# Fused attention and MoE: where in a tile's turn the scores of its last 128 keys are issued

## The chip, the cores and the metric

The kernel runs on one core of a Trainium2 chip. The metric is the device time of one execution in microseconds (us), as the median of several runs. The profile is of one execution. The engines are named as the profile names them: PE is the matrix engine, PEld its weight loads, DVE the vector engine, ACT the scalar engine, POOL the GpSimd, SP the queue that issues most transfers.

## The reference

Three layers follow one another: attention over queries that were pooled in pairs, then two MoE-like layers on its output. The change is in the attention.

```
B, H, S, D = 4, 8, 1152, 64
q_pool = q.reshape(B, H, S // 2, 2, D).mean(axis=3)          # 576 queries
scores = scale * np.matmul(q_pool, k.transpose(0, 1, 3, 2))  # 576 x 1152
scores = scores - np.max(scores, axis=-1, keepdims=True)
attn = np.exp(scores)
attn = attn / (np.sum(attn, axis=-1, keepdims=True) + 1e-09)
out = np.matmul(attn, v)
```

## The kernel before

**Tiles.** The 32 pairs of batch and head are taken two at a time: 16 steps p, each with two heads h. A step has 9 tiles t of 128 query rows. Tiles 0 to 7 are four blocks of 128 queries of each head; tile 8 holds the last 64 queries of both heads. So 144 tiles g follow each other, with p = g // 9 and t = g % 9.

**One tile.** `scores` (L74) multiplies a tile's queries with the first 1024 of its 1152 keys: two products of 512 keys, one on the upper and one on the lower 64 rows of PE, into a tile `s` of two PSUM banks, of which there are two. `scores_rest` (L88) does the last 128 keys, on the upper 64 rows, into a tile `r` of one bank, of which there is one. `maximum` (L101) has DVE take the extreme of `s` (L105) and then of `r` together with it (L112). `exps` (L115) has ACT read `r` (L123), which frees it once the row's sum has been read out, and then `s` (L125), and write the exponentials `aw_e`. `transp` (L130) turns these on PE, in 64-row halves: part 0 is 10 transposes (5 key blocks), part 1 is 8 (4 blocks). Both parts use the one tile `t` in PSUM, so part 1 can begin only when DVE has copied part 0 out (`back`, L155), and part 0 of the next tile only when ACT has copied part 1 out (L153). `push` and `av` (L194, L221) multiply the turned exponentials with the values (L203), a chunk of 8 or 12 products in each tile's turn, from a list that is filled half a step later; 8 of 9 turns of a step have such a chunk. `sums` and `sums_turn` (L159, L168) invert a half step's row sums on DVE (L164, L165) and turn them on PE (L171) into free columns of `r`. A multiplication in fp32 shows in the trace as two passes, so a score product is two rows.

**Order.** Nothing is scheduled by a tool: each piece is entered with `at(time, ...)`, where the whole part of the time is the tile's turn and the fraction the place in it, and the list is sorted and issued in that order. Each engine executes its own instructions in that order. In the turn of tile g PE has so far:

1. .0 `scores` of g
2. .15 part 1 of the transposes of g-2
3. .2 `scores_rest` of g
4. .25 the turned sums, in two turns of nine
5. .5 a chunk of the values' products
6. .98 part 0 of the transposes of g-1

DVE has in the same turn the copy of part 0 of g-2 (.1, L155), finished outputs (.11, L211, L213), one step of a background job that splits MoE weights (.12), inverted sums (.13), and the extremes of g (.6). ACT has the exponentials of g-1 (.15), the copy of part 1 of g-2 (.4), and a background step (.42). POOL adds pairs of query rows for the next step (L71, L72) as soon as their transfer has landed.

Of the kernel before, what the change touches and what calls it, by code (L numbers as in the profile page):

```python
# [29 lines left out]
def attention(tc, nc, ap, cst, xT, bg, hooks):  # L30
# [5 lines left out]
    with ExitStack() as ctx:  # L36
# [197 lines left out]
        def at(time, f, *a):  # L234
            events.append((time, len(events), f, a))
# [6 lines left out]
        for g in range(NT):  # L242
            p, t = divmod(g, NTL)
            at(g, scores, g)
            at(g + .2, scores_rest, g)
            at(g + .6, maximum, g)
            at(g + 1.15, exps, g)
            at(g + 1.98, transp, g, 0)
            at(g + 2.1, back, g, 0, "v")
            at(g + 2.15, transp, g, 1)  # L250
            at(g + 2.4, back, g, 1, "a")
            if t == 3:
                at(g + 2.13, sums, p, 0)
                at(g + 2.25, sums_turn, p, 0, g + 2)
                at(g + 4.05, spread, p, 0)
                at(g + 3.45, push, p, 0)
            if t == 8:
                at(g + 2.13, sums, p, 1)
                if g + 2 < NT:
                    at(g + 2.25, sums_turn, p, 1, g + 2)  # L260
                else:
                    at(g + 2.25, sums_last, p, 1)
                at(g + 4.05, spread, p, 1)
                at(g + 3.45, push, p, 1)
            if p + 1 < NP:
                if t in (0, 1):
                    at(g + .3 if p else g + 1.3, load_qk, p + 1, t)
                if t in (3, 4):
                    at(g + .3, prep, p + 1, t - 3, nc.gpsimd)
                if t == 6:  # L270
                    at(g + .3, load_v, p + 1)
            if t % 9 not in (3, 4, 5) and g > 3:
                at(g + .12, step, "v")
                at(g + .42, step, "a")
# [922 lines left out]
def fused(tc, q, k, v, w_in, w_sp, b_sp, w_out, w_g, w1, w2, consts, out):  # L1197
# [7 lines left out]
    with ExitStack() as ctx, tc.manual_schedule():  # L1205
# [6 lines left out]
        hooks = {"raw": lambda: m1.begin_v(keep([128, 4096], F32R, "wv").rearrange("p (n k c) -> p n k c", n=2, k=4)),  # L1212
                 "S": m1.begin, "x1": m1.begin_x1, "T": lambda: m1.split_x(0, m1.x0), "end": m1.begin_u}
        attention(tc, nc, ap, cst, xT, bg, hooks)
        bgp.close()
        tab = Pool(ctx.enter_context(tc.tile_pool(name="tab", bufs=1, side="right")), "tab")
# [77 lines left out]
```

## Time and profile before

| what | value |
|---|---|
| three runs, us | 1066.67, 1064.51, 1060.57; median 1064.51 |
| the profiled execution, us | 1063.56, its span 1061.7 |
| attention, by the first and last of its products | about 6 to 510 us of the span |
| PE busy over the span | 1008.2 us, 95% |
| DVE, ACT, POOL busy | 748.7 (71%), 595.3 (56%), 225.5 us (21%) |
| L137 on PE (transposes) | x2592, PEld idle before them 193.1 us, of which 130.3 behind DVE L155 |
| L95 on PE (scores of the last 128 keys, tiles 0 to 7) | x256, 57.2 us |
| PE clock | full in 300 to 500 us, 0.98 from 100 to 300 us |

A busy share is an average over stages: from 6 to 510 us the attention runs, behind it the other layers with other limits. The profile models where a matrix product ends, so on PE the starts of neighbouring rows say more than the lengths. A row of the timeline merges instructions of one group; its start is that of the first, its length reaches to the end of the last.

### The profile page before, as it was taken

The page shows a single profiled execution, that of the slowest core. Times are in us where ns is not written, and L with a number is a line of the kernel's source. Part 1 is how long each engine was busy: PE and PEld are TensorE (multiplying, and loading weights), DVE is VectorE, ACT ScalarE, POOL GpSimd, SP SyncE. Part 2 cuts the span into 40 slices and gives each one's busy share as a digit, 9 for nine tenths or more (in the row PEclk, how much of TensorE's full clock was granted, in tenths as well). Part 3 has the DMA queues.
Part 4 walks back from the last instruction along what each step waited for, and adds up shares of the span by engine and source line. Part 5 has one row for each costly group of instructions (what it writes and reads, how often), then busy time and mean ns, then how long its engine had stood idle before and what let it go on. Part 6 is the DMA issues. An engine that isn't in the chain of part 4 may idle for free.

```text
span 1061.7 us, 19763 instructions
## 1 busy us (share of the span) xinstructions
PE 1008.2 (95%) x7532; PEld 679.5 (64%) x7532; DVE 748.7 (71%) x1361; ACT 595.3 (56%) x1172; POOL 225.5 (21%) x189
## 2 busy tenths in 40 slices
PE   6899999999999999999879999999999999999997
PEld 3444444444544444444668988998777777777775
DVE  6787787878777787776498414232688787888884
ACT  4666666666666666666323322122277777777773
POOL 1111111111101111100355312231212321213111
PEclk9999999999999999999979999999999999999999
DMA  4444223443433343331512111001745142112840
GB/s 164 139 132 134 80 86 133 135 135 131 133 87 116 95 136 125 125 120 68 204 56 80 34 65 59 1 1 39 248 181 201 37 148 92 40 41 83 312 176 28
DMA packets 50495, 116.75 MB, mean 110 GB/s; under 512 B 8986, under 2 KB 21586, under 8 KB 48856
## 3 DMA queue, kind: packets, MB, share of 16 engines
q1 hardware_dynamic: 46672, 104.37, 29.0%
q0 software_dynamic: 3680, 11.02, 3.2%
q8 instruction: 62, 1.02, 0.4%
q14 instruction: 41, 0.34, 0.1%
q10 hardware_dynamic: 40, 0.01, 0.0%
HBM read 165.61 MB, written 19.47 MB: 174 GB/s over the span
## 4 chain that ended last, share of the span: by engine, by line
PE 75%; DVE 10%; DMA 7%; issue 4%; ACT 2%; POOL 1%; SPq 0%; POOLq 0%; DVEq 0%; ACTq 0%
PE ps_av L203 15%; PE ps_t L137 11%; PE ep_yp L1074 8%; PE ps_s L82 8%; PE ep_hp L1041 6%; DMA er_x<-x,tab_gi 4%; PE m_ps_v L626 4%; PE m_ps_u L574 4%; PE m_ps_u L560 3%; PE m_ps_v L519 3%; PE ep_hp L1034 3%; PE ps_r L95 3%; DVE aw_mx L105 2%; PE ps_s L85 2%; DMA ao_qr<-in_q 1%
## 5 line engine op out<-in xcount | busy, mean ns | idle before, releaser
L137 PEld LDWEIGHTS ps_t<-keep_ident,aw_e 64*128 64x128 f32 x2592 | 104.0, 140 | 193.1 <-DVE aw_et L155 130.3
L105 DVE TENSOR_REDUCE aw_mx<-ps_s 128x1 f32<-128x1024 f32 x144 | 174.7, 1213 | 8.3 <-ACT aw_e L125 2.5
L155 DVE COPY aw_et<-ps_t 128x640 f32<-128x640 f32 x144 | 118.5, 823 | 81.8 <-PE ps_t L137 81.5
L203 PE MATMUL ps_av<-aw_et,aw_v 128*64 128x320 f32 (+1 forms) x1152 | 168.9, 420 | 0.0
L125 ACT ACTIVATE aw_e<-ps_s,aw_mx 128x1024 f32<-128x1024 f32 x144 | 159.2, 1106 | 0.0
L137 PE MATMUL ps_t<-keep_ident,aw_e 64*128 64x64 f32 x2592 | 143.5, 235 | 15.8 <-DVE aw_et L155 12.0
L82 PE MATMUL ps_s<-ao_k,ao_q 64*128 64x512 f32 x512 | 141.7, 632 | 7.2 <-DMA ao_k<-in_k 6.0
L123 ACT ACTIVATE aw_e<-ps_r,aw_mx 128x128 f32<-128x128 f32 x144 | 53.0, 368 | 130.4 <-DVE aw_junk L112 130.4
L153 ACT ACTIVATE aw_et<-ps_t 128x512 f32<-128x512 f32 x144 | 86.0, 597 | 54.7 <-PE ps_t L137 53.4
L372 DVE TENSOR_TENSOR eb_w2l<-er_r,eb_w2h 128x1024 fp32r<-128x1024 f32 x88 | 103.5, 1217 | 4.2 <-ACT eb_w2h L368 4.1
L203 PEld LDWEIGHTS ps_av<-aw_et,aw_v 128*64 128x64 f32 x1152 | 72.0, 137 | 49.0 <-issue 4.1
L372 DVE TENSOR_TENSOR eb_w1l<-er_r,eb_w1h 128x1024 fp32r<-128x1024 f32 x66 | 78.7, 1221 | 33.6 <-ACT eb_w1h L368 33.6
L368 ACT ACTIVATE eb_w2h<-er_r 128x1024 fp32r<-128x1024 f32 x88 | 88.7, 1068 | 0.6 <-PE ep_yp L1074 0.3
L368 ACT ACTIVATE eb_w1h<-er_r 128x1024 fp32r<-128x1024 f32 x66 | 67.8, 1071 | 17.4 <-DMA er_r<-in_w 13.2
L372 POOL TENSOR_TENSOR bg_l<-bg_e,bg_h 128x256 fp32r<-128x256 f32 x16 | 11.6, 728 | 296.5 <-ACT bg_h L368 296.5
L1074 PE MATMUL ep_yp<-eb_w2h,ew_hth 128*128 128x512 f32 x176 | 71.2, 404 | 0.2 <-ACT ew_hth L368 0.2
L1074 PE MATMUL ep_yp<-eb_w2h,ew_htl 128*128 128x512 f32 x176 | 70.2, 399 | 0.2 <-DVE ew_htl L372 0.2
L1074 PE MATMUL ep_yp<-eb_w2l,ew_hth 128*128 128x512 f32 x176 | 69.1, 392 | 0.0
L1080 POOL DMA_INDIRECT out<-ew_y,tab_si x22 | 22.4, 1017 | 206.8 <-DVE ew_y L1079 183.2
L112 DVE TENSOR_SCALAR_CACHE_REDUCE aw_junk<-ps_r,aw_mx 128x128 f32<-128x128 f32 x144 | 49.9, 346 | 14.4
L71 POOL TENSOR_TENSOR ao_qr<-ao_qr 128x576 f32<-128x576 f32 x30 | 43.2, 1442 | 72.6 <-DMA ao_qr<-in_q 72.1
L95 PE MATMUL ps_r<-ao_k,ao_q 64*128 64x128 f32 x256 | 57.2, 304 | 0.0
(240 smaller groups left out, 1908.5 us busy)
## 6 DMA issues: line engine op xcount, KB each, us to landing
er_r<-in_w SPq DMA_DIRECT2D x45, 2048.0 KB
ao_qr<-in_q SPq DMA_DIRECT2D x32, 576.0 KB
ao_k<-in_k SPq DMA_DIRECT2D x32, 320.0 KB
aw_v<-in_v SPq DMA_DIRECT2D x16, 576.0 KB
xT<-aw_xo SPq DMA_DIRECT2D x16, 288.0 KB
bg_raw<-in_w_in SPq DMA_DIRECT2D x16, 256.0 KB
aw_rb<-rdram SPq DMA_DIRECT2D x64, 64.0 KB
er_r<-in_w SPq DMA_DIRECT2D x16, 256.0 KB
```

The source lines that it names most:

```text
L82: nc.tensor.matmul(d["s"][:, i, :], r["q", h][rows, 128 * n:128 * n + 128], r["k", h][rows, 0:512], start=True, stop=True)
L95: nc.tensor.matmul(d["r"][:, 0:128], r["q", h][rows, 128 * n:128 * n + 128], r["k", h][rows, 512:640], start=True, stop=True)
L105: nc.vector.tensor_reduce(out=m[:, 0:1], in_=d["s"], op=ALU.min, axis=AX.XY)
L125: nc.scalar.activation(out=e[:, 0:8, :].rearrange("p k c -> p (k c)"), in_=d["s"].rearrange("p i c -> p (i c)"), func=AF.Exp, bias=d["m"][ ...
L137: nc.tensor.transpose(t[:, i, 64 * (k - k0):64 * (k - k0) + 64], E[g]["e"][o, k, :], ident[o, o])
L153: nc.scalar.activation(out=o, in_=i, func=AF.Copy)
L155: nc.vector.tensor_copy(o, i)
L203: nc.tensor.matmul(box["t"][64 * h:64 * h + 64, 0:n], v[:, h, k, :], et[:, k, h, 0:n], start=k == 0, stop=k == 8)
L368: nc.scalar.activation(out=hi, in_=src, func=AF.Copy)
L372: (nc.gpsimd if eng_lo == "p" else nc.vector).tensor_tensor(out=lo, in0=src, in1=hi.bitcast(F32), op=ALU.subtract)
L1041: nc.tensor.matmul(pt[c], xT[xi][:, 128 * k:128 * k + 128], W1[wi][:, k, 512 * c:512 * c + 512], start=False, stop=todo[c] == 0)
L1074: nc.tensor.matmul(pt, hT[hi][:, c, 128 * o:128 * o + 128], W2[wi][:, f, :], start=f == 0 and (hi, wi) == (0, 0), stop=f == 7 and (hi, wi) ...
```

## The change

One number: in the list of places, `scores_rest` of tile g moves from .2 to .14, so that it is issued before the second part of the transposes (.15) and not behind it.

```
         for g in range(NT):
             p, t = divmod(g, NTL)
             at(g, scores, g)
-            at(g + .2, scores_rest, g)
+            at(g + .14, scores_rest, g)
             at(g + .6, maximum, g)
             at(g + 1.15, exps, g)
             at(g + 1.98, transp, g, 0)
             at(g + 2.1, back, g, 0, "v")
             at(g + 2.15, transp, g, 1)
```

Only PE's order changes. On PE, two whole turns in the second step (ps_s and ps_r are `s` and `r`, ps_t the transposes' tile, ps_av the values' products; the number at a name's end only counts tiles):

```order
 L82 MATMUL ps_s_571<-ao_k_10_156,ao_q_12_229 128x512 x2
-L137 MATMUL ps_t_579<-keep_ident_65,aw_e_544 128x64 x8
-L95 MATMUL ps_r_591<-ao_k_10_156,ao_q_12_229 128x128
+L95 MATMUL ps_r_579<-ao_k_10_156,ao_q_12_229 128x128
+L137 MATMUL ps_t_581<-keep_ident_65,aw_e_546 128x64 x8
 L203 MATMUL ps_av_551<-aw_et_294,aw_v_88 64x320 x4
-L137 MATMUL ps_t_605<-keep_ident_65,aw_e_588 128x64 x10
+L137 MATMUL ps_t_605<-keep_ident_65,aw_e_590 128x64 x10
```

The scores of the last keys now stand directly behind the other scores, and the eight transposes directly ahead of the values' products; the ten transposes at the turn's end stay.

On PE, the turn of a tile 8 in the first step, whose queries come from two heads and whose products use 64 columns instead of 128:

```order
 L85 MATMUL ps_s_382<-ao_k_2_82,ao_q_5_90 64x512
 L85 MATMUL ps_s_382<-ao_k_4_86,ao_q_6_95 64x512
-L137 MATMUL ps_t_389<-keep_ident_65,aw_e_357 128x64 x8
-L98 MATMUL ps_r_401<-ao_k_2_82,ao_q_5_90 64x128
-L98 MATMUL ps_r_401<-ao_k_4_86,ao_q_6_95 64x128
+L98 MATMUL ps_r_389<-ao_k_2_82,ao_q_5_90 64x128
+L98 MATMUL ps_r_389<-ao_k_4_86,ao_q_6_95 64x128
+L137 MATMUL ps_t_392<-keep_ident_65,aw_e_359 128x64 x8
 L203 MATMUL ps_av_321<-aw_et_138,aw_v_88 64x256 x4
```

Here the products of 64 columns, which stood on both sides of the transposes, now stand together.

On PE, a turn with turned sums (L171) and without values' products, in the second step:

```order
 L82 MATMUL ps_s_469<-ao_k_10_156,ao_q_12_229 128x512 x2
-L137 MATMUL ps_t_481<-keep_ident_65,aw_e_438 128x64 x8
-L95 MATMUL ps_r_494<-ao_k_10_156,ao_q_12_229 128x128
-L171 MATMUL ps_r_494<-keep_ident_65,aw_rs_40_478 5x128
-L137 MATMUL ps_t_516<-keep_ident_65,aw_e_491 128x64 x10
+L95 MATMUL ps_r_481<-ao_k_10_156,ao_q_12_229 128x128
+L137 MATMUL ps_t_483<-keep_ident_65,aw_e_440 128x64 x8
+L171 MATMUL ps_r_481<-keep_ident_65,aw_rs_40_478 5x128
+L137 MATMUL ps_t_516<-keep_ident_65,aw_e_493 128x64 x10
```

The turned sums keep their place ahead of the ten transposes; they now follow the eight transposes directly.

## Rows read from the trace of the kernel before

**Rows 1.** Page, part 1, PE's share, and part 2, PE's granted clock in 40 slices.
```profile
PE 1008.2 (95%) x7532; PEld 679.5 (64%) x7532; DVE 748.7 (71%) x1361; ACT 595.3 (56%) x1172; POOL 225.5 (21%) x189
...
PEclk9999999999999999999979999999999999999999
```
**Rows 2.** Page, part 5: PE's transposes; weight loads and matmuls, idle time before them.
```profile
L137 PEld LDWEIGHTS ps_t<-keep_ident,aw_e 64*128 64x128 f32 x2592 | 104.0, 140 | 193.1 <-DVE aw_et L155 130.3
...
L137 PE MATMUL ps_t<-keep_ident,aw_e 64*128 64x64 f32 x2592 | 143.5, 235 | 15.8 <-DVE aw_et L155 12.0
```
**Rows 3.** Timeline of a turn, t=4: start us, length us, instruction, [idle before <-releaser].
```profile
300.74 0.37 ACT L123 ACTIVATE aw_e<-ps_r,aw_mx 128x128 f32<-128x128 f32 x1 [0.74 <-DVE aw_junk L112]
...
300.79 0.53 PE L137 MATMUL ps_t<-keep_ident,aw_e 64*128 64x64 f32 x10
...
301.15 1.08 PE L82 MATMUL ps_s<-ao_k,ao_q 64*128 64x512 f32 x4
301.36 0.82 DVE L155 COPY aw_et<-ps_t 128x640 f32<-128x640 f32 x1 [0.71 <-PE ps_t L137]
...
302.23 0.32 PEld L137 LDWEIGHTS ps_t<-keep_ident,aw_e 64*128 64x128 f32 x8 [0.83 <-DVE aw_et L155]
302.24 0.46 PE L137 MATMUL ps_t<-keep_ident,aw_e 64*128 64x64 f32 x8
...
302.53 0.44 PE L95 MATMUL ps_r<-ao_k,ao_q 64*128 64x128 f32 x2
...
302.90 1.30 PE L203 MATMUL ps_av<-aw_et,aw_v 128*64 128x320 f32 x8
```
**Rows 4.** Timeline of PE, the same turn, short windows: the second passes alone.
```profile
301.63 0.59 PE L82 MATMUL ps_s<-ao_k,ao_q 64*128 64x512 f32 x2
...
302.70 0.27 PE L95 MATMUL ps_r<-ao_k,ao_q 64*128 64x128 f32 x1
```
**Rows 5.** Timeline of PE and PEld in a later layer: products, then transposes.
```profile
860.18 0.63 PE L1041 MATMUL ep_hp<-eb_w1h,ew_xtl 128*128 128x512 f32 x2
860.65 0.62 PE L1041 MATMUL ep_hp<-eb_w1l,ew_xth 128*128 128x512 f32 x2
861.11 0.60 PE L1022 MATMUL ep_xt<-keep_ident,er_x 128*128 128x128 f32 x4
```
**Rows 6.** Timeline of PE, turn of a tile 8.
```profile
314.49 0.53 PE L137 MATMUL ps_t<-keep_ident,aw_e 64*128 64x64 f32 x10
...
314.94 1.09 PE L85 MATMUL ps_s<-ao_k,ao_q 64*64 64x512 f32 x8
...
315.96 0.46 PE L137 MATMUL ps_t<-keep_ident,aw_e 64*128 64x64 f32 x8
...
316.35 0.44 PE L98 MATMUL ps_r<-ao_k,ao_q 64*64 64x128 f32 x4
...
316.72 1.08 PE L203 MATMUL ps_av<-aw_et,aw_v 128*64 128x256 f32 x8
```
**Rows 7.** Timeline, end of t=1 and turn of t=2.
```profile
323.70 0.27 PE L171 MATMUL ps_r<-keep_ident,aw_rs 128*5 128x128 f32 x1 [0.23 <-DVE aw_rs L165]
...
325.56 0.19 ACT L123 ACTIVATION_READ_ACCUMULATOR aw_e<-ps_r,aw_mx 128x1 f32 x1
...
325.99 0.46 PE L137 MATMUL ps_t<-keep_ident,aw_e 64*128 64x64 f32 x8 [0.65 <-DVE aw_et L155]
...
326.66 0.76 PE L203 MATMUL ps_av<-aw_et,aw_v 128*64 128x320 f32 x4
```
**Rows 8.** Timeline, turn of t=7.
```profile
311.93 0.82 DVE L155 COPY aw_et<-ps_t 128x640 f32<-128x640 f32 x1
...
312.38 0.19 ACT L123 ACTIVATION_READ_ACCUMULATOR aw_e<-ps_r,aw_mx 128x1 f32 x1
...
313.47 1.08 PE L203 MATMUL ps_av<-aw_et,aw_v 128*64 128x256 f32 x8
```
**Rows 9.** Timeline, t=1 of another step; then busy times and clock of a stretch.
```profile
104.17 1.45 POOL L71 TENSOR_TENSOR ao_qr<-ao_qr 128x576 f32<-128x576 f32 x1 [4.97 <-DMA ao_qr<-in_q]
...
104.28 1.36 DVE L164 SCALAR_TENSOR_TENSOR aw_rs<-aw_sum 128x5 f32<-128x5 f32 x1
...
108.10:111.50 3.40, 3.29 (x18) 1.69 (x18) 2.15 (x5) 2.48 (x6) 0.52 (x1) 0.50 0.10 29
```
**Rows 10.** One line of the kernel, L164: duration ns min/median/max.
```profile
L164 DVE SCALAR_TENSOR_TENSOR aw_rs<-aw_sum x32: 147/153/1360, 23.3 to 504.4; 128x4 f32<-128x4 f32 x16, 128x5 f32<-128x5 f32 x16
```

More of the change, by code (lines that the diff above doesn't have):

```diff
@@ L244, in attention @@
             at(g, scores, g)
-            at(g + .2, scores_rest, g)
+            at(g + .14, scores_rest, g)
             at(g + .6, maximum, g)
```

## Prediction

> **What bounds the kernel now.** I read the page's shares first: PE is busy 95% of the span at full clock nearly throughout [rows 1], so time must come from PE's own row or from waits that the row hides. Then the costliest groups. The transposes' weight loads stood idle 193.1 us, 130.3 of them behind L155, DVE's copy of the first ten transposes; their matmuls by the profile only 15.8, 12.0 of them behind L155 [rows 2]. The two differ because the ends of PE's rows are modelled: the scores' row reaches as far as the next row. Which is right is read from starts in a plain turn [rows 3, 4]. The scores start at 301.15, their second pass at 301.63, so a pass is 0.48 us apart, and the second should be through about 302.1. The eight transposes start at 302.24. Their copy L155 ends at 301.36 + 0.82 = 302.18, and the weight load starts 0.05 behind it. So PE stands still for some 0.1 to 0.2 us ahead of the eight transposes in a turn where the page counts almost nothing. L155 cannot come earlier: it itself waited 0.71 us for the ten transposes of 300.79.
>
> In 9 turns of a step I find three sorts. Plain ones, like rows 3: t=0, 3, 4, 5 and 6, and t=8 with another shape. Late ones, where DVE had too much before L155: t=2 (its transposes waited 0.65 us [rows 7]) and t=7 (L155 starts directly behind DVE's last instruction, with no idle time [rows 8]). And t=1, which has no values' products and ends on the turned sums, for which PE waits on DVE [rows 7].
>
> **The change, part by part.** It removes and adds no instruction and no transfer; on DVE, ACT, POOL and SP the order is as before. On PE one product of two passes goes ahead of eight transposes. I compare the stretch from the scores' start to the values' products.
>
> *Plain turn, before:* 302.90 - 301.15 = 1.75 us [rows 3].
>
> *Plain turn, after:* the first pass is 0.48. The second I take from tile 8, where the copy is not what is waited for: 315.96 - 314.94 = 1.02 for both passes there, less 0.48, less the change of shape. That change costs 0.09: the scores follow the ten transposes by 0.45 in tile 8 [rows 6] and by 0.36 in rows 3. So 0.45. The rest's first pass is 302.70 - 302.53 = 0.17; its second, by columns 128 of 512, is 0.11 [rows 4]. The transposes start at 0.48 + 0.45 + 0.17 + 0.11 = 1.21, about 0.06 less if the rest's weights load under the scores' second pass, as they cannot behind short transposes, and its first pass too takes 0.11: 1.15. That is after the copy, which allows 1.09, so the copy is no longer waited for. Eight transposes last 302.53 - 302.24 = 0.30, and the change of shape ahead of the values' products, which before stood behind the rest, is 0.09; with the weights loaded ahead the first pair is some 0.02 shorter: 0.37. In all 1.52, a gain of 0.23 us. Bounds: nothing overlaps and each pass takes 0.48 and 0.17 (1.30 + 0.39 = 1.69, gain 0.06), or the transposes start at the copy's earliest and follow directly (1.09 + 0.34 = 1.43, gain 0.32). I take 0.23, near the better end, because the one place in the trace where transposes directly follow long products shows no gap: L1041's pairs start 0.47 apart and the transposes 0.46 behind the last pair [rows 5].
>
> *A wait that the change brings forward:* the rest needs `r`, which ACT frees with L123 of the tile before. In a plain turn L123 ends at 300.74 + 0.37 = 301.11, and with the sum's readout 0.2 later; the rest would be issued at about 302.1, or 0.23 earlier when turns shrink. Some 0.6 us to spare; behind it stand the eight transposes, the copy L153 and the values' products, which all would be late with it. In late turns there is nothing to spare. *t=2:* the readout of L123 ends at 325.56 + 0.19 = 325.75; the rest follows at about 325.80, the transposes 0.28 later at 326.08 (before 325.99), the values' products 0.37 later at 326.45 against 326.66: gain 0.21, less 0.03 if the rest's second pass is long. I take 0.18; bounds 0.10 and 0.30. *t=1* gains nothing of its own, as L171 waits for DVE's sums [rows 7] wherever the rest stands. *t=6 and 7 together:* t=6 gains 0.23, but DVE gets no faster, so t=7 meets DVE and ACT where they were: readout of L123 at 312.57, rest 312.62, transposes 312.90, values 313.27 against 313.47 [rows 8]. For both 0.17; bounds 0.10 and 0.30. *t=8:* before 316.72 - 314.94 = 1.78; after 0.48 + 0.45 + 0.28 + 0.09 + 0.39 = 1.69, as one change of shape goes and one stays: 0.09; bounds 0.03 and 0.15.
>
> *Sum of a step:* t=0, 3, 4, 5 give 4 x 0.23 = 0.92, t=1 and 2 0.18, t=6 and 7 0.17, t=8 0.09: 1.36 us. Fifteen steps look alike; in the first, turns have no values' products and wait on ACT, DVE and transfers, and I count nothing. 15 x 1.36 = 20.4. The layers behind attention start from its end and shift with it. From the profiled execution, 1063.56 us (0.95 below the median of the runs), that gives 1043.2.
>
> **A rule on shapes.** The rest and the transposes both stand as 64*128 [rows 3], tile 8's products as 64*64 [rows 6], and only there does the trace show the 0.09. The Trainium skill (TensorEngine Tiling, Key Properties) says that the array drains when its tiling mode changes, not when only the tile within a mode does. By that the plain turn has no drain between rest and transposes, as I count; if each such pair cost a drain all the same, 4 x 0.09 x 15 = 5.4 us of the gain would go. No run here shows a rest directly ahead of transposes.
>
> **Rivals.**
>
> *Little overlap.* The page's own PE row has only 12.0 us of idle time behind L155 [rows 2], and part of it is in late turns such as t=2. If that is the true idle time, or the passes take their full spacing, plain turns gain 0.06 to 0.15 and a step about 0.65: 15 x 0.65 = 10, so 1053.5. For it: the page; against it: rows 3 and 4, where the passes do not fill the stretch.
>
> *DVE or ACT take over.* PE arrives earlier, but meets copies and extremes that are no faster, and turns keep their length: 1062. For it: DVE sets t=1, 2 and 7 already. Against it: in the plain turn L155 had waited 0.71 us for PE [rows 3], three times what PE gains.
>
> *Slower, by POOL.* DVE's L164 usually takes 0.15 us, but 1.36 at most [rows 10]: POOL's L71 began 0.11 us ahead of it, ran to 105.62, and L164 ended at 105.64. PE had waited, and then the clock stood at 0.50, 1.2 of 2.4 GHz, for 3.40 us [rows 9]. That is 1.2 us for the wait and at most 1.7 for the clock, 2.9 a time. L71 starts when a transfer has landed; shorter turns move L164 against it. With 10 of the 32 places of L164 hit anew the time is 1043.2 + 29 = 1072.2; it is slower than before from 8 new hits on. Against it: a start 0.1 to 0.2 us earlier takes L164 out from behind L71 in the case shown. The Trainium skill (SBUF, Who interferes with whom) states a lock between DVE and GpSimd: whichever starts first holds the shared ports for its whole instruction, against a DVE instruction with two inputs. The trace agrees, by those two ends.
>
> **How the numbers follow.** The forecast 0.65 (its own range 1033 to 1049, from 4 x 0.32 + 0.30 + 0.30 + 0.15 = 2.03 us a step at best to about 1.0); little overlap 0.17; take-over 0.10; POOL 0.08. The range to hold it 8 times in 10 reaches from 1033 to 1056, which takes in the little overlap. About 0.5%, 5.3 us, is what a measurement of this kernel can tell from no change: faster 0.65 + 0.17 = 0.82, same 0.10, slower 0.08.
>
> **What would show it.** In a plain turn the eight transposes should start 1.1 to 1.2 us after the scores with PEld's wait behind L155 nearly gone, and the values' products 1.45 to 1.55 after the scores against 1.75. In t=2 the weight load of the rest, not the transposes, should wait, and for ACT's L123. t=1 and 2 together should lose 0.2 us. DVE's wait ahead of L155 should shrink by as much as a turn. I am wrong if the transposes still start behind L155, if the rest waits for ACT in plain turns, or if L164 is long in many steps.

## The result and the profile after

| | before | changed |
|---|---|---|
| median of 6 runs, us | 1065.42 (1060.57 to 1069.78) | 1039.22 (1032.73 to 1041.95) |
| profiled execution, us | 1063.56 | 1039.24 |
| first step (first scores of step 0 to those of step 1) | 32.40 | 38.60 |
| steps 1 to 15, to the end of the last values' product | 471.76 | 440.40 |
| from the first product of the next layer on | 549.6 | 550.0 |

The ratio to before is 0.9738, 95% interval 0.9709 to 0.9767. Forecast were 1043.2 us and a range of 1033 to 1056.

The page of the changed kernel, PE's share and groups of part 5, answers to [rows 1, 2]. The weight loads of the transposes stood idle 193.1 us before, 130.3 behind the copy L155. Now they stand 66.4 us, most of it behind the other copy, L153, and the rest's weight loads have a wait of their own, for L123:

```profile
PE 981.8 (95%) x7532; PEld 695.3 (67%) x7532; DVE 745.6 (72%) x1361; ACT 594.2 (57%) x1172; POOL 228.0 (22%) x189
...
L137 PEld LDWEIGHTS ps_t<-keep_ident,aw_e 64*128 64x128 f32 x2592 | 109.6, 141 | 66.4 <-ACT aw_et L153 40.2
...
L95 PEld LDWEIGHTS ps_r<-ao_k,ao_q 64*128 64x128 f32 x256 | 47.2, 194 | 83.6 <-ACT aw_e L123 52.5
```

A plain turn of the changed kernel, from its timeline, answers to [rows 3]:

```profile
287.14 0.52 PE L137 MATMUL ps_t<-keep_ident,aw_e 64*128 64x64 f32 x10
...
287.50 1.08 PE L82 MATMUL ps_s<-ao_k,ao_q 64*128 64x512 f32 x4
...
287.71 0.82 DVE L155 COPY aw_et<-ps_t 128x640 f32<-128x640 f32 x1 [0.43 <-PE ps_t L137]
...
287.99 0.19 PEld L95 LDWEIGHTS ps_r<-ao_k,ao_q 64*128 64x128 f32 x1 [0.24 <-ACT aw_e L123]
288.41 0.38 PE L95 MATMUL ps_r<-ao_k,ao_q 64*128 64x128 f32 x2
...
288.59 0.46 PE L137 MATMUL ps_t<-keep_ident,aw_e 64*128 64x64 f32 x8
...
288.98 1.30 PE L203 MATMUL ps_av<-aw_et,aw_v 128*64 128x320 f32 x8
```

The eight transposes start 1.09 us after the scores, as before, and as before that is 0.06 us behind the end of their copy (287.71 + 0.82 = 288.53): L155 still sets their first start. What has changed is that the rest (288.41) is already in front of them, in the time in which PE stood still. The rest's weight load waits 0.24 us for L123, but ends well before its products are due, so this wait holds nothing up. From scores to values it is 288.98 - 287.50 = 1.48 us against 1.75. DVE's idle time ahead of L155 fell from 0.71 to 0.43, by the turn's gain.

The late turn t=2, from a timeline of the same kernel, answers to [rows 7]. The weight load of the rest is now what waits, for ACT, and the transposes start 1.72 after the scores as they did before (325.99, behind scores at 324.27, the line of before below); but the values' products follow 0.47 behind them and not 0.67:

```profile
324.27 1.08 PE L82 MATMUL ps_s<-ao_k,ao_q 64*128 64x512 f32 x4
```
```profile
309.46 1.08 PE L82 MATMUL ps_s<-ao_k,ao_q 64*128 64x512 f32 x4
...
310.75 0.19 ACT L123 ACTIVATION_READ_ACCUMULATOR aw_e<-ps_r,aw_mx 128x1 f32 x1
310.99 0.29 PEld L95 LDWEIGHTS ps_r<-ao_k,ao_q 64*128 64x128 f32 x2 [1.28 <-ACT aw_e L123]
...
311.18 0.27 PE L137 MATMUL ps_t<-keep_ident,aw_e 64*128 64x64 f32 x1
...
311.65 0.49 PE L203 MATMUL ps_av<-aw_et,aw_v 128*64 128x320 f32 x2
```

Turn by turn, medians of steps 1 to 14, each turn from the start of its scores to that of the next (us):

| turn t | 0 | 1 | 2 | 3 | 4 | 5 | 6 | 7 | 8 | sum |
|---|---|---|---|---|---|---|---|---|---|---|
| before | 3.56 | 2.62 | 3.97 | 3.34 | 3.34 | 4.08 | 3.13 | 3.24 | 3.16 | 30.44 |
| changed | 3.29 | 2.62 | 3.78 | 3.07 | 3.07 | 3.81 | 2.93 | 3.25 | 2.99 | 28.81 |
| gain | 0.27 | 0.00 | 0.19 | 0.27 | 0.27 | 0.27 | 0.20 | -0.01 | 0.17 | 1.63 |
| forecast | 0.23 | with t=2 | 0.18 | 0.23 | 0.23 | 0.23 | with t=7 | 0.17 | 0.09 | 1.36 |

Fifteen times 1.63 is 24.5 us. The steps gained 471.76 - 440.40 = 31.4. Most of the rest is POOL's: in the profile before, three steps were 2.7, 2.0 and 1.1 us longer than a usual one, those with an L164 of 1.36 us [rows 9, 10], and behind the first two of them PE's clock fell for 3.4 us; in the profile after no L164 lasted over 0.16, and the clock did not fall in these steps. About 1 us of the 31.4 is left without a cause. The view of the line, in the changed kernel:

```profile
L164 DVE SCALAR_TENSOR_TENSOR aw_rs<-aw_sum x32: 152/153/160, 27.5 to 479.3; 128x4 f32<-128x4 f32 x16, 128x5 f32<-128x5 f32 x16
```

Against that the first step took 6.2 us more. I had counted nothing there. The timeline of its turns shows two things. Before, the scores at 13.45 lasted 2.02 us, those from 16.95 on 1.08; and the ten transposes between them waited 0.35 us for L153:

```profile
13.45 2.02 PE L82 MATMUL ps_s<-ao_k,ao_q 64*128 64x512 f32 x4
...
16.59 0.53 PE L137 MATMUL ps_t<-keep_ident,aw_e 64*128 64x64 f32 x10 [0.35 <-ACT aw_et L153]
...
16.95 1.08 PE L82 MATMUL ps_s<-ao_k,ao_q 64*128 64x512 f32 x4
```

In the changed kernel the scores from 14.07 to 26.53 lasted 2.02 us, twice as long, in four turns. So PE's clock was at the lower of its two levels, 1.2 and not 2.4 GHz. The trace's record of the clock begins only when it first rises, 15.9 us from the timeline's zero before and 29.6 us in the changed kernel; what went before is read from the scores' length. In these turns there are no values' products, and where the rest stood in front of the ten transposes PE now stands idle 0.70 us:

```profile
17.64 0.80 PE L137 MATMUL ps_t<-keep_ident,aw_e 64*128 64x64 f32 x10 [0.70 <-ACT aw_et L153]
...
26.53 2.02 PE L82 MATMUL ps_s<-ao_k,ao_q 64*128 64x512 f32 x4
...
30.46 1.08 PE L82 MATMUL ps_s<-ao_k,ao_q 64*128 64x512 f32 x4
```

The clock did not stay up. Within the first step it fell once more, for 3.4 us before and for 6.8 us in the changed kernel; in these stretches, the first of the profile before, the third figure from the end is the granted clock:

```profile
32.98:36.39 3.41, 3.41 (x26) 1.16 (x24) 1.52 (x6) 1.55 (x4) 0.00 (x0) 0.50 0.00 1
36.39:43.22 6.83, 6.73 (x48) 3.69 (x49) 3.98 (x8) 3.29 (x8) 0.00 (x0) 0.50 0.22 80
```

So the first step had PE at the lower clock for 13.4 us before and for 30.4 us after the change.

Whether the order did that, or chance, is the first question of the experiments. The others: is L164 really held by POOL's L71; what sets the plain turn now; and does the new place pay in the late turns too.

### The profile page after: what moved, and what is told of

Same layout as the page of the kernel before. It is cut to its first block, busy times and chain, and to the rows that moved or that the text cites. A ratio compares the mean times of both kernels' runs of the same rounds, so it can differ in the third digit from the quotient of the medians.

```text
span 1037.4 us, 19763 instructions
## 1 busy us (share of the span) xinstructions
PE 981.8 (95%) x7532; PEld 695.3 (67%) x7532; DVE 745.6 (72%) x1361; ACT 594.2 (57%) x1172; POOL 228.0 (22%) x189
## 4 chain that ended last, share of the span: by engine, by line
PE 74%; DVE 11%; DMA 6%; issue 5%; ACT 3%; POOL 0%; SPq 0%; ACTq 0%; DVEq 0%; POOLq 0%
PE ps_av L203 15%; PE ps_t L137 9%; PE ep_yp L1074 9%; PE ps_s L82 8%; PE ep_hp L1041 7%; PE m_ps_v L626 5%; DMA er_x<-x,tab_gi 4%; PE m_ps_u L574 4%; PE m_ps_v L519 3%; PE ep_hp L1034 3%; PE m_ps_u L560 3%; PE ps_r L95 3%; DVE aw_mx L105 2%; PE ps_s L85 2%; PE ep_ht L1059 1%
## 5 line engine op out<-in xcount | busy, mean ns | idle before, releaser
L155 DVE COPY aw_et<-ps_t 128x640 f32<-128x640 f32 x144 | 118.4, 822 | 57.7 <-PE ps_t L137 57.4
L137 PEld LDWEIGHTS ps_t<-keep_ident,aw_e 64*128 64x128 f32 x2592 | 109.6, 141 | 66.4 <-ACT aw_et L153 40.2
L137 PE MATMUL ps_t<-keep_ident,aw_e 64*128 64x64 f32 x2592 | 148.6, 235 | 5.3 <-ACT aw_et L153 3.0
L123 ACT ACTIVATE aw_e<-ps_r,aw_mx 128x128 f32<-128x128 f32 x144 | 52.9, 367 | 121.3 <-DVE aw_junk L112 121.3
L153 ACT ACTIVATE aw_et<-ps_t 128x512 f32<-128x512 f32 x144 | 85.9, 596 | 39.3 <-PE ps_t L137 35.9
L95 PEld LDWEIGHTS ps_r<-ao_k,ao_q 64*128 64x128 f32 x256 | 47.2, 194 | 83.6 <-ACT aw_e L123 52.5
L95 PE MATMUL ps_r<-ao_k,ao_q 64*128 64x128 f32 x256 | 53.8, 291 | 8.3 <-ACT aw_e L123 7.6
```

Source lines behind the costliest of these rows:

```text
L95: nc.tensor.matmul(d["r"][:, 0:128], r["q", h][rows, 128 * n:128 * n + 128], r["k", h][rows, 512:640], start=True, stop=True)
L137: nc.tensor.transpose(t[:, i, 64 * (k - k0):64 * (k - k0) + 64], E[g]["e"][o, k, :], ident[o, o])
L153: nc.scalar.activation(out=o, in_=i, func=AF.Copy)
L155: nc.vector.tensor_copy(o, i)
```

## Experiments

Eleven runs followed, two of them of the changed kernel itself, in three groups, each group on one chip and timed beside the kernel before. Ratios are to the kernel before, with 95% intervals. "Rise" is the moment at which the trace first records PE's clock at its full level, counted from the first operation; that stands 0.25 us behind the zero of the timelines, so there a rise reads 0.25 us higher.

**The old place in the first step.** The edit to the changed kernel:

```
-            at(g + .14, scores_rest, g)
+            at(g + (.2 if g < NTL else .14), scores_rest, g)
```

> The changed kernel, but the first step (tiles 0 to 8) keeps the old place of the rest's scores. In the profile of the changed kernel the first step lasted 38.6 us against 32.4 before, at the lower clock until 29 us against 16 us. Theory A (the new order itself keeps the clock down in the first step, where turns have no values' products): the first step is back near 32.4 us, the clock full by 16 to 17 us, the time about 6 us below the changed kernel's 1039.2, so 1033. Rival B (when the clock rises is chance from run to run, whatever the order): the time stays at 1039, and the first step may last anything from 32 to 39 us.

Median 1033.85 us, ratio 0.9694 (0.9657 to 0.9730); the rise came at 16.6 us, the first step took 31.4. As theory A has it, but the interval overlaps the changed kernel's, and one profile cannot tell the order from chance.

**The new place in the first step alone.** The edit to the kernel before:

```
-            at(g + .2, scores_rest, g)
+            at(g + (.14 if g < NTL else .2), scores_rest, g)
```

> The kernel before, with the new order in the first step alone (tiles 0 to 8). Theory A: the first step lasts some 38.5 us and the time is 6 us above the kernel before, 1071.5. Rival B: no difference from the kernel before, 1065.4.

Median 1068.26 us, ratio 1.0008 (0.9974 to 1.0041): the 6 us of theory A lie outside. The rise came at 16.3 us and the first step took 32.3, in spite of the new order. So A fails as I had put it: the order does not always keep the clock down.

**Products before the first scores.** The edit to the changed kernel:

```
         load_v(0)
+        warm(nc, ps([128, 2, 512], F32, "s", bufs=2), ident, 12)
```

> The changed kernel, with 24 transposes and 36 small products of the identity issued on PE ahead of the first scores, while the first queries are still being fetched (a tile of the scores' buffer takes them and is overwritten). If the first step is long only because PE is at the lower clock there, the clock rises earlier, the first step falls below 34 us and the time to 1033 or lower. If the new order makes the first step longer at full clock too, the first step stays above 36 us and the time at 1039. If the clock falls again before the scores run, also 1039.

Median 1043.08 us, ratio 0.9772 (0.9736 to 0.9808): a miss of my own making. At the lower clock the 60 products took from 2.71 to 14.6 us, and the first scores came 8.6 us later:

```profile
2.71 1.54 PE L1190 MATMUL ps_s<-keep_ident 64*128 64x64 f32 x24 [2.71 <-DMA keep_ident<-in_consts]
4.05 5.32 PE L1193 MATMUL ps_s<-keep_ident 64*128 64x64 f32 x48
9.31 5.38 PE L1195 MATMUL ps_s<-keep_ident 128*128 128x64 f32 x24
14.62 2.08 PE L82 MATMUL ps_s<-ao_k,ao_q 64*128 64x512 f32 x4
```

Its one use: though PE issued without a gap from 2.7 us on, the rise came no earlier than 16.9. The first step, from these later first scores, lasted 31.9 us.

**One operand for the sums.** The edit to the kernel before:

```
-            nc.vector.scalar_tensor_tensor(out=rs[:, 0:n], in0=s[:, 0:n, 0], scalar=1e-9, in1=s[:, 0:n, 1], op0=ALU.add, op1=ALU.add)
+            nc.vector.tensor_reduce(out=rs[:, 0:n], in_=s[:, 0:n, :], op=ALU.add, axis=AX.X)
```

> The kernel before (old order), with the sums' first instruction L164 made from one operand: a sum over the last axis of the 2 partial sums in place of an addition of two tensors; the added 1e-9 is left out. Theory C (the 1.36 us of L164 are a wait for POOL's L71, which holds what a DVE instruction with two SBUF operands needs): no row of it lasts over 0.3 us, even where L71 runs beside it; three long turns go, and the time falls by up to 5.8 us to about 1060. Rival D (L164 waits for its operands, ACT's sums, or for the transfer that L71 also waited for): long rows stay, and the time stays at 1065.

Median 1059.45 us against 1068.01 on that chip, ratio 0.9928 (0.9899 to 0.9957). In this timeline L71 again began just before L164, as in [rows 9], by 0.07 us against 0.11 there; the view of the line has all 32:

```profile
103.10 1.42 POOL L71 TENSOR_TENSOR ao_qr<-ao_qr 128x576 f32<-128x576 f32 x1 [5.01 <-DMA ao_qr<-in_q]
103.17 0.16 DVE L164 TENSOR_REDUCE aw_rs<-aw_sum 128x5 f32<-128x10 f32 x1
```
```profile
L164 DVE TENSOR_REDUCE aw_rs<-aw_sum x32: 146/151/156, 23.9 to 499.4; 128x4 f32<-128x8 f32 x16, 128x5 f32<-128x10 f32 x16
```

With one operand L164 runs beside L71, as theory C has it. But not all of the lost time came back: steps 1 to 15 took 467.85 us against 471.76 in the profile before, 3.9 less and not 5.8. In two steps t=1 was still 1.15 and 1.01 us too long, for L71 now met L336, a background instruction of two operands just ahead of L164, which lasted 1.57 and 1.42 us instead of 0.41:

```profile
254.69 1.40 POOL L71 TENSOR_TENSOR ao_qr<-ao_qr 128x576 f32<-128x576 f32 x1 [4.65 <-PE ps_s L82]
254.80 1.57 DVE L336 SCALAR_TENSOR_TENSOR bg_e<-bg_raw,bg_e 128x256 int32<-128x256 int32 x1
```

The 8.6 us between the medians are more than that; no trace shows where the other executions gained them.

**The changed kernel again**, unchanged, beside the next three.

> The changed kernel itself, once more, beside the other three on one chip, for a second look at its first step. So far the clock rose to full at 16 to 17 us in five profiles, with the old and with the new order in the first step, and at 29 us in one, that of the changed kernel. Theory B (chance): it rises at about 16 us this time, the first step lasts near 32 us, and the profiled execution takes about 1033; over its runs the times lie in two groups some 6 us apart. Theory A (the new order): 29 us again, a first step of 38 us.

Median 1036.80 us, ratio 0.9724 (0.9677 to 0.9772). The rise came at 20.0 us and the first step took 33.6: neither theory's figure. The times, 1031 to 1046, do not fall into two groups.

**The old place in late turns.** The edit to the changed kernel:

```
-            at(g + .14, scores_rest, g)
+            at(g + (.2 if t in (2, 7) else .14), scores_rest, g)
```

> The changed kernel with the old place of the rest's scores in the two turns where DVE is late, t=2 and t=7, of every step. Theory (the new place pays there too, by taking the rest from behind the transposes, although the rest now waits for ACT): t=2 goes from 3.78 back to 3.98 us, t=7 becomes 0.2 longer, so 0.4 us a step, 15 steps, 6 us: 1045. Rival (in late turns the gain is nothing, since the rest waits for ACT about as long as the transposes waited for DVE): 1039, turns as in the changed kernel.

Median 1041.26 us, ratio 0.9754 (0.9718 to 0.9790). The difference to the changed kernel beside it, 4.5 us, is within the intervals; the turns decide. t=2 took 3.97 us against 3.78, t=7 3.45 against 3.25, so a step is 0.39 us longer, as the theory has it. In its timeline of t=2 the transposes wait for L155 and the rest stands behind them again:

```profile
75.87 1.08 PE L82 MATMUL ps_s<-ao_k,ao_q 64*128 64x512 f32 x4
...
77.47 0.46 PE L137 MATMUL ps_t<-keep_ident,aw_e 64*128 64x64 f32 x8 [0.52 <-DVE aw_et L155]
77.77 0.44 PE L95 MATMUL ps_r<-ao_k,ao_q 64*128 64x128 f32 x2
78.14 1.29 PE L203 MATMUL ps_av<-aw_et,aw_v 128*64 128x320 f32 x7
```

**Half of the values' products ahead of the rest in t=2.** The edit to the changed kernel:

```
-            for k0, k1 in ((0, 2), (2, 4), (4, 6), (6, 9)):
+            for k0, k1 in ((0, 1), (1, 2), (2, 4), (4, 6), (6, 9)) if c else ((0, 2), (2, 4), (4, 6), (6, 9)):
...
-                at(g + 3.45, push, p, 1)
+                at(g + 3.12, push, p, 1)
+                at(g + 3.135, av)
```

> The changed kernel, with half of the values' products of the turn t=2 put ahead of the rest's scores there, where PE now waits some 0.6 us for ACT to free r (to have them, the list is filled some tenths of a turn earlier). If that wait is what sets the turn, t=2 falls from 3.78 to about 3.5 us, where the copy L153, held up on ACT, becomes what the next transposes wait for: 0.3 us a step, 4.5 us in all, 1034.5. If DVE's lateness sets t=2 and 3 together whatever PE does, t=3 grows by what t=2 gains, and the time stays at 1039. It is slower if the two further changes of shape, 0.18 us, are not hidden: up to 1042.

Median 1033.76 us, ratio 0.9678 (0.9638 to 0.9718), 3 us below the changed kernel beside it, within the intervals. The turn went where expected, from 3.78 to 3.49, and what its end waits for is now L153:

```profile
77.23 1.08 PE L82 MATMUL ps_s<-ao_k,ao_q 64*128 64x512 f32 x4
...
78.24 0.76 PE L203 MATMUL ps_av<-aw_et,aw_v 128*64 128x320 f32 x4
...
79.59 0.76 PE L203 MATMUL ps_av<-aw_et,aw_v 128*64 128x320 f32 x4
79.70 0.60 ACT L153 ACTIVATE aw_et<-ps_t 128x512 f32<-128x512 f32 x1
80.35 0.39 PEld L137 LDWEIGHTS ps_t<-keep_ident,aw_e 64*128 64x128 f32 x10 [0.57 <-ACT aw_et L153]
```

In five of the steps 1 to 14 t=3 gave 0.12 to 0.25 us of it back; its median stayed at 3.07.

**Three edits together:** the first, the one of the sums and the one of the values' products.

> The changed kernel with three further edits: the old place of the rest's scores in the first step, the inverted sums made by a sum over one operand (the added 1e-9, which a float32 sum of at least 1 cannot hold, is left out), and half of the values' products of t=2 ahead of the rest. If the three add up: the first step near 32 us (about 4 us below the changed kernel on average), no long L164 (about 1 us, as the changed kernel has few), 4.5 us from t=2: 1030. If the split does nothing: 1034.

Median 1032.61 us, ratio 0.9696 (0.9657 to 0.9736), where 1030 was expected: the lowest median, but by no interval better than the changed kernel. Its profiled execution took 1029.29, with the rise at 16.7 us, a first step of 31.0 and t=2 at 3.48.

**The waits of the first step filled.** The edit to the changed kernel:

```
+        def cover():
+            t = ps([128, 512], F32, "av")
+            for i in range(6):
+                nc.tensor.transpose(t[:, 64 * i:64 * i + 64], ident[0:64, :], ident[0:64, 0:64])
...
             at(g + 2.15, transp, g, 1)
+            if g < 4:
+                at(g + 2.155, cover)
```

> The changed kernel, with six transposes of the identity, into the values' bank that is unused then, behind the second transposes of the first four tiles. In these turns of the first step there are no values' products, and since the change PE stands idle there for 0.70 us until ACT's copy L153 is through, where the rest's scores stood before. So far the clock rose at 15.7, 16.6, 16.7 and 17.1 us with the old order in the first step, and at 16.3, 18.7, 20.0, 23.9 and 29.3 us with the new. Theory (the uncovered wait for L153 keeps PE's clock down longer): filled, the clock rises by 17 us, the first step lasts 31 to 33 us, the time is some 3 us below the changed kernel's. Rival (the moment is chance): anything from 16 to 29 us, the time as the changed kernel's, 1037 to 1039.

The rise came at 15.6 us, the first step took 31.8. Median 1034.82, ratio 0.9688 (0.9661 to 0.9716). In its timeline the ten transposes wait 0.32 us for L153, where they waited 0.70. But the clock had already risen, at 15.8 us of this timeline, when the first filling transpose ran at 16.10, so the filling did not bring the rise:

```profile
16.10 0.53 PE L222 MATMUL ps_av<-keep_ident 64*128 64x64 f32 x6
16.31 0.60 ACT L153 ACTIVATE aw_et<-ps_t 128x512 f32<-128x512 f32 x1 [1.02 <-PE ps_t L137]
...
16.96 0.53 PE L137 MATMUL ps_t<-keep_ident,aw_e 64*128 64x64 f32 x10 [0.32 <-ACT aw_et L153]
17.32 1.08 PE L82 MATMUL ps_s<-ao_k,ao_q 64*128 64x512 f32 x4
```

**The changed kernel a third time**, on that chip.

> The changed kernel a third time, beside the one with filled waits and on the same chip, for one more moment of the clock's rise. Theory: later than 17 us, a first step of 33 to 39 us. Rival (chance): anything.

The rise came at 20.1 us, the first step took 33.9; two runs, 1034.31 and 1034.60, ratio 0.9689 (0.9649 to 0.9730). The filled kernel is not faster than this one.

All profiles by the order in the first step; the third column is the time from the first scores to those of step 1 that PE spent at the lower clock, before the rise and in later falls:

| order in the first step | rise, us | at the lower clock, us | first step, us |
|---|---|---|---|
| old (before; first edit; one operand; three edits) | 15.7, 16.6, 17.1, 16.7 | 13.4, 11.0, 11.5, 11.1 | 32.4, 31.4, 31.4, 31.0 |
| new (changed, three times; first step alone; halves) | 29.3, 20.0, 20.1, 16.3, 23.9 | 30.4, 17.7, 17.9, 13.6, 24.9 | 38.6, 33.6, 33.9, 32.3, 36.6 |
| new but for t=2 and 7 (old place in late turns) | 18.7 | 19.8 | 34.8 |
| new, waits filled | 15.6 | 12.7 | 31.8 |
| new, the rest doubled (below) | 17.2 | 14.8 | 33.6 |
| new, products before the first scores | 16.9 | 12.8 | 31.9 |

But for the doubled rest, every first step is 27.0 us and 0.38 us for each us at the lower clock, to within 0.4, with either order (an estimate from this table). So the new order made the first step longer only where PE was longer at the lower clock: with 13.6 us at the lower clock it took 32.3, the old one with 13.4 us 32.4.

**The rest twice.** The edit to the changed kernel, tiles 0 to 7:

```
-                nc.tensor.matmul(d["r"][:, 0:128], r["q", h][rows, 128 * n:128 * n + 128], r["k", h][rows, 512:640], start=True, stop=True)
+                for _ in range(2):
+                    nc.tensor.matmul(d["r"][:, 0:128], r["q", h][rows, 128 * n:128 * n + 128], r["k", h][rows, 512:640], start=True, stop=True)
```

> The changed kernel, with the rest's scores of tiles 0 to 7 computed twice in a row (the same products into the same place). In plain turns of the changed kernel the rest starts 0.91 us after the scores, takes 0.17, and the transposes start at 1.09, where the copy L155 also allows them. If the copy sets them and PE had time left, the transposes move by less than the 0.22 us that the second rest adds; by the 0.06 us that the weight load could have started earlier, to 1.25. If PE alone sets them, they move by the full 0.22, to 1.31. A step becomes 1.0 to 1.4 us longer, the time 15 to 20 us.

Median 1061.74 us, ratio 0.9931 (0.9903 to 0.9959): 27.3 us above the changed kernel beside it, where 15 to 20 were expected. A step was 1.3 us longer by medians, as expected, which is 19.5 us in fifteen; in the profile 5.3 us more came from the layers behind, where PE was at the lower clock for 40.7 us against 27.7. Its timeline of a plain turn (line numbers from L96 on are higher by one):

```profile
295.13 1.07 PE L82 MATMUL ps_s<-ao_k,ao_q 64*128 64x512 f32 x4
...
295.34 0.82 DVE L156 COPY aw_et<-ps_t 128x640 f32<-128x640 f32 x1 [0.65 <-PE ps_t L138]
...
296.05 0.38 PE L96 MATMUL ps_r<-ao_k,ao_q 64*128 64x128 f32 x2
...
296.22 0.27 PE L138 MATMUL ps_t<-keep_ident,aw_e 64*128 64x64 f32 x1
296.27 0.27 PE L96 MATMUL ps_r<-ao_k,ao_q 64*128 64x128 f32 x1
...
296.33 0.22 PE L138 MATMUL ps_t<-keep_ident,aw_e 64*128 64x64 f32 x1
296.38 0.27 PE L96 MATMUL ps_r<-ao_k,ao_q 64*128 64x128 f32 x1
296.39 0.50 PE L138 MATMUL ps_t<-keep_ident,aw_e 64*128 64x64 f32 x6
...
296.82 0.76 PE L204 MATMUL ps_av<-aw_et,aw_v 128*64 128x320 f32 x4
```

From scores to values it is 296.82 - 295.13 = 1.69 us, 0.21 more than in the changed kernel: the full price of the second rest. So PE has no time left over in the plain turn, and the copy no longer holds up the values' products. Yet the first transpose still starts at 1.09, neither at 1.25 nor at 1.31 as the expectation had it: again 0.06 us behind the end of the copy (295.34 + 0.82 = 296.16). Both can be true, because half of the transposes use the lower 64 rows and can start, when the copy lets them, between the passes of the rest, which uses the upper 64; the others follow the rest. That the rows at 296.22 and 296.33 are of the lower half is argued from the kernel, since the view does not name the half.

## Why the prediction was right, point by point

**What bounded the kernel** was read rightly: PE stood still ahead of the eight transposes, in turns where the page's PE row counted next to nothing. The weight loads' 130.3 us behind L155 were nearer the truth than the matmuls' 12.0 [rows 2]; a gain of 1.63 us a step could not have come out of 12.0.

**The plain turn** was mis-sized a little: 0.23 us forecast, 0.27 measured, within the bounds of 0.06 and 0.32. I let the transposes start at 1.15, behind both passes of the rest and with the copy no longer waited for. They start at 1.09, beside its second pass and 0.06 us behind the end of L155. So to the letter a sign of being wrong that I had named, transposes that still start behind L155, is there; what the copy has lost is its hold on the values' products, which the doubled rest moved by its full price. There is no sign of a drain between rest and transposes: 0.18 us lie between their starts, less than the two passes of 0.11 that stand there. The same rows refute the 0.09 us a turn that the sentence on shapes put against the forecast, and the rival of little overlap, 1053.5.

**t=1** (nothing) came as worked out, and so did the sum of **t=2** (0.18, measured 0.19), with the wait for L123 where it was put. Inside t=2 two errors cancel: the transposes start 1.72 us after the scores, where the sum had 326.08 - 324.27 = 1.81, and the values' products 0.47 behind them and not 0.37. **t=6 and 7**: 0.17 forecast, 0.19 by medians. t=6 gained 0.20 and not 0.27 for a reason I did not name: the values' products of 295.93 start 0.46 us behind the transposes and not 0.39, and 0.06 behind the end of L213, the last reader of the bank they write. The timeline of the changed kernel:

```profile
295.47 0.46 PE L137 MATMUL ps_t<-keep_ident,aw_e 64*128 64x64 f32 x8
295.66 0.21 DVE L213 TENSOR_TENSOR aw_xo<-ps_av,aw_rb 128x64 f32<-128x64 f32 x1
295.93 1.08 PE L203 MATMUL ps_av<-aw_et,aw_v 128*64 128x256 f32 x8
```

t=7 gained nothing, as DVE's lateness allows. Both late turns need the new place all the same: with the old one a step is 0.39 us longer. **t=8**: 0.09 forecast, 0.17 measured, outside its bounds of 0.03 and 0.15; by medians the rest and its change of shape took 0.32 us there where the sum had 0.37, and the scores' passes 0.91 for 0.93.

**The first step** is the term that failed: counted at nothing, it cost 6.2 us in the profiled execution. My list of what stands behind the rest named the values' products, but not the turns without any, where the rest itself had covered PE's wait for L153. The wait grew from 0.35 to 0.70 us, but it is the clock that the 6.2 us follow: 17.0 us more at the lower clock, at 0.38 each, make 6.5. Whether the order keeps the clock down is not settled. Four profiles with the old order rose at 15.7 to 17.1 us, six with the new at 16.3 to 29.3; by first steps that is some 3 us on average. Against it stands that the clock rose in two profiles, with the new order in the first step alone and with the waits filled, before the first lengthened wait or the first filling transpose. Up to there PE had the same instructions in the same order as in the three profiles of the changed kernel, which rose at 20.0 us and later, so chance has a part at least. And the new order in the first step alone showed no loss in time, filling the waits no gain.

**POOL** was the rival on the slower side, and it went the other way: the three meetings of the profile before were gone, 5.8 us that I had not put into the sum. The sentence against the rival had said why, that an earlier start takes L164 out from behind L71, but put no gain to it. For L164 the mechanism, two operands on DVE against an L71 that started first, is borne out by the kernel with one operand. The price of 2.9 us a meeting was too high on the whole: 2.7, 2.0 and 1.1 in the profile before, and 1.2 for each of two long L164 in the kernel with the new order in the first step alone, where the clock did not fall behind them. So the forecast, 1043.2 against 1039.2, holds three misses of which two nearly cancel: steps 4.1 us too small (15 x 0.27), POOL 5.8 not counted, the first step 6.2 not counted. That the total came within 4.0 us is in part luck.

**DVE or ACT take over**: not in the plain turn (the doubled rest moved it by its full price), but in t=1 and t=7, which gained nothing, as the prediction allowed.

## What to carry to other kernels

Where an instruction waits for a copy, look for independent work that stands behind it on the same engine and can go in front; size it by the starts of neighbouring rows and by the weight loads' idle time, since the matmul row hides the wait. Then go through the turns in which the moved piece had itself covered another wait, above all the first turns of a loop, where the usual work is missing. And a single long row of a short instruction is worth tracing to what ran beside it: giving L164 one operand instead of two took it out of POOL's way. Then look at its neighbours as well: in that kernel L336 was twice the long one instead, with L71 beside it, and cost 1.2 and 1.0 us.

## What the runs showed of the hardware that I had not expected

Products on the upper 64 rows of PE and transposes, by the kernel's order those of the lower 64, run beside each other in fine grain: rest passes at 296.27 and 296.38, transposes at 296.22 and 296.33. A DVE addition of two operands took 1.36 us instead of 0.15 when POOL's L71 had begun 0.11 us earlier, a sum over one operand 0.16 when it had begun 0.07 earlier. And PE's clock was first full at 16.9 us even when PE had issued products without a gap since 2.7 us. In two profiles with the same order of instructions in the first step it was first full at 16.3 and at 29.3 us.
